# Wq's first half loaded in two slices on two queues, the later slices issued behind the fourth zero matmul

## The chip, the cores and the metric

The kernel runs on one core of one Trainium2 chip. The metric is the device time of one execution in microseconds (us). The profile shows one such execution: its span runs from the first to the last instruction of the program, and the execution's own time is a little longer than the span.

## The reference

Two branches share one input x of 2048 rows and 512 columns, and a gate mixes them:

```python
x = A_x                                               # [1, 2048, 512], bfloat16
g = sigmoid((x * gate_w).sum(-1, keepdims=True))

# branch a: attention, 32 heads of 16, over 8 keys at distances 0, 2, ..., 14 behind each row
q, k, v = split(x @ wqkv)                             # wqkv [512, 1536]
logits  = einsum("bhsd,bhswd->bhsw", q, gathered_k) * 16 ** -0.5
a = einsum("bhsw,bhswd->bhsd", softmax(masked(logits)), gathered_v) @ wo

# branch b: an MLP over the rows
h = layernorm(x)
u = gelu(einsum("bsd,sf->bdf", h, w1) + b1)           # w1 [2048, 1792]
b = (einsum("bdf,fs->bds", u, w2) + b2).transpose     # w2 [1792, 2048]

out = g * a + (1 - g) * b
```

## The kernel before

All work is written as operations with what they read and write, an estimated duration, and one of five queues (SP, POOL, ACT, DVE, PE: SyncE, GpSimd, ScalarE, VectorE, TensorE). A planner (`_Sched`, lines 76 to 279) then puts the operations of each queue into a fixed order by these estimates and works out the semaphore waits. A DMA is an operation of the queue that issues it: an issue time on the queue, and a landing that the planner takes from bytes, or from a due time written by hand (`lands`, line 499). `deps` are waits for completion; `order` and `after` bind only the order in which things are issued. `chain` (line 956) writes parts of the order out by hand, VectorE's among them (line 969).

**TensorE's stages.** Zero matmuls first (`warm1`, line 552: nine of 128x512 into PSUM bank 7, released by a VectorE memset). Then the projections of x to Q, K and V. They contract over 512 columns in four steps (dt 0 to 3), need x transposed (XT, in four blocks of 512 rows, sb 0 to 3) as the moving operand, and columns of Wqkv as the stationary one. One group of four matmuls fills one PSUM bank for one of four column sets (dl 0 to 3), and ScalarE copies the bank out (`ev_...`, lines 651 and 654). The first block of rows is treated apart (lines 656 to 667): Q's four groups go to banks 0 to 3, and K's to banks 4 to 7. Q's are cut by what has landed: dt 0 and 1 over the first 384 rows (XS = 384), dt 0 and 1 over the other 128, dt 2 and 3 over all 512; K's follow whole. After them come the groups of blocks 1 to 3 (`pj_...`, line 678), then V's, all in one order by `after=[last_main[0]]`. All of these matmuls are line 643.

Between them stand bursts of line 698 (`qkr_...`): they sum, over a head's columns, the products q times shifted k that VectorE makes (`qkm_...`, line 690), into banks 4 to 7. `qkr_1_1` reads what `qkm_1_1_0` writes. Behind the projections follows `gz` (line 618), the gate's matmuls, which read a VectorE transpose (`t_b`, line 536); then the MLP's two halves (`ph2`, line 853, and `ph3`, line 890), each ordered behind the one before and behind `gz`; near the end `ws_3` (line 807) and the output projection (`wo`, line 907).

**VectorE's order at the start** is written by hand: memset, an indicator matrix, then the layernorm statistics of row tiles 0 to 3 (`ln1_...`, line 570), the products `qkm_0_0_0` and `qkm_0_1_0`, and so on in turns up to `qkm_1_1_0`, two small operations, `t_b`, and the rest. `ln1_0` needs the first quarter of x in its own layout (`d_x0`).

**The loads at the start.** ACT's queue: Wq's dt 0 and 1 (256 KB, `wq01`), Wq's dt 2 and 3 when the first has landed (`wq23`), Wk whole (512 KB). SP's queue: the transposing DMA of rows 0 to 383 of x (`ld_xt0`, line 484), that of rows 384 to 511 (`xt0b`), the one of block 1 (`ld_xt(1)`, line 477) when `xt0b` has landed, then x's rows 0 to 511 and 512 to 1023 (`ld_x`), blocks 2 and 3 transposed, the rest of x, Wv, w1, wo and the biases. `init_dmas` lists SP's loads, and `throttle()` makes a load wait for the one five places before it in that list.

Of the kernel before, what the change touches and what calls it, by code (L numbers as in the profile page):

```python
# [5 lines left out]
BF16 = mybir.dt.bfloat16  # L6
# [7 lines left out]
D = 512  # L14
# [14 lines left out]
XS = 384  # L29
# [310 lines left out]
def bass_gated_mix__sliding_local_dilated__mixer_token_mlp__prompt_kernel(nc, A_x, A_wqkv, A_wo, B_x, B_w1, B_b1, B_w2, B_b2, gate_w, out, dbg=None):  # L340
    with contextlib.ExitStack() as es:
        block = es.enter_context(nc.Block())
        view, pview, off, total = _views(nc, es)
        ps = es.enter_context(nc.psum_tensor("ps", [128, 8, 512], FP32))
# [34 lines left out]
        OUTS = view("OUTS", BF16, [(D, 4), (1, D)])  # L379
# [51 lines left out]
        A = sch.add  # L431
# [16 lines left out]
        init_dmas = []  # L448
# [15 lines left out]
        def ld_w(tn, d0, n, q="sp"):  # L464
            ds = sch.dsem("wqkv%d_%d" % (tn, d0))
            op = sch.dma(q, mk_dma(WQKV[:, d0:d0 + n, tn * D:(tn + 1) * D], wqkv_v[:, d0:d0 + n, tn * D:(tn + 1) * D]),
                         n * 128 * D * 2, ds, writes=["wqkv%d_%d" % (tn, dt) for dt in range(d0, d0 + n)],
                         deps=throttle() if q == "sp" and n == 4 else [], after=prev_dma() if q == "sp" else [],
                         issue=0.65 if n == 4 else 0.45, name="d_wp%d_%d" % (tn, d0))
            if q == "sp":  # L470
                init_dmas.append(op)
            return op
# [8 lines left out]
        def ld_xt0(s0, s1):  # L481
            ds = sch.dsem("xt0_%d" % s0)
            dst = XT[:, :, s0:s1]
            op = sch.dma("sp", lambda e: e.dma_start_transpose(dst, x2d[s0:s1, :]), (s1 - s0) * D * 2, ds, issue=1.25,
                         writes=["xt_%d" % t for t in range(s0 // 128, s1 // 128)], after=prev_dma(), name="d_xt0_%d" % s0)
            init_dmas.append(op)
            return op

        wq01 = ld_w(0, 0, 2, "act")
        ld_xt0(0, XS)  # L490
        xt0b = ld_xt0(XS, 512)
        wq23 = ld_w(0, 2, 2, "act")
        wq23.deps.add(wq01)
        wk = ld_w(1, 0, 4, "act")
        wk.order.add(wq23)
        ld_xt(1)
        init_dmas[-1].deps.add(xt0b)
        for op_, t_ in ((wq01, 3.0), (init_dmas[0], 4.5), (xt0b, 5.1), (wq23, 5.9), (wk, 7.4), (init_dmas[-1], 9.5)):
            op_.lands = t_
        ld_x(0, 4)  # L500
        ld_x(4, 4)
# [20 lines left out]
        for g in range(4):  # L522
            d_wo = sch.dma("sp", mk_dma(psub(WO, 32 * g, 32, 0, [(D, 4), (1, D)]), wov[g]), 32 * 4 * D * 2, ds_wo,
                           writes=["wo%d" % g], deps=throttle(), name="d_wo%d" % g)
# [6 lines left out]
        for i_, (v_, n_) in enumerate(((B_b1, NFT), (B_b2, NST), (gate_w, 4))):  # L531
            vr = v_.rearrange("(t q j) -> q t j", q=4, j=32)
            for q_ in range(4):
                sch.dma("sp", mk_dma(psub(BR, 32 * q_, n_, 32 * i_, [(1, 32)]), vr[q_]), n_ * 64, ds_b, reads=["br"],
                        writes=["br_%d_%d" % (i_, q_)], deps=throttle(), after=prev_dma(), name="d_b_%d_%d" % (i_, q_), issue=0.45)
        A("dve", lambda e: e.transpose(out=BT, in_=BR), 0.2, reads=["br_%d_%d" % (i_, q_) for i_ in range(3) for q_ in range(4)],
          writes=["gwc"], name="t_b")
        A("act", lambda e: e.activation(out=B1C, in_=BT[:, 0, 0:NFT], func=AF.Copy), 0.2, reads=["gwc"], writes=["b1c"], name="b1c")
        A("act", lambda e: e.activation(out=B2C, in_=BT[:, 1, 0:NST], func=AF.Copy), 0.2, reads=["gwc"], writes=["b2c"], name="b2c")

        WARM = view("OUTS", BF16, [(1, D)], extra=0)
        A("dve", lambda e: e.memset(WARM, 0.0), 0.2, writes=["outs0"], name="warm0")

        def f_warm(n):
            def fn(e):
                ins = None
                for _ in range(n):
                    ins = e.matmul(ps[:, 7, :], lhsT=WARM[:, 0:128], rhs=WARM, start=True, stop=True)
                return ins
            return fn  # L550

        last_tx = A("pe", f_warm(9), 4.0, reads=["outs0"], writes=["lg7_0", "lg7_1"], name="warm1", prio=-100)

        ALLXT = ["xt_%d" % t for t in range(NST)]

# [11 lines left out]
        for hf in range(2):  # L567
            t0 = 8 * hf
            for t in range(t0, t0 + 8):
                A("dve", (lambda t_: (lambda e: e.bn_stats(out=ST6[:, t_, :], in_=X[:, t_, :])))(t), 0.59,  # L570
                  reads=["x%d" % t], writes=["st6_%d" % t], name="ln1_%d" % t, prio=0)
# [13 lines left out]
              reads=["zc%d" % hf], writes=["sd%d" % hf], name="ln_sqrt%d" % hf, prio=0)  # L585
            A("dve", (lambda t0_: (lambda e: e.reciprocal(out=cols(RSTD, t0_, 8), in_=cols(SD, t0_, 8))))(t0), 0.25,
              reads=["sd%d" % hf], writes=["rstd%d" % hf], name="ln_rstd%d" % hf, prio=0)
# [68 lines left out]
        tnames = ["q", "k", "v"]  # L656
        first = [(tn, dl) for tn in range(2) for dl in range(4)]
        fbn = [["acc%d" % b] for b in range(4)] + [["lg%d_0" % b, "lg%d_1" % b] for b in range(4, 8)]
        for (b0, d0, d1, s0, s1) in ((0, 0, 2, 0, XS), (0, 0, 2, XS, 512), (0, 2, 4, 0, 512), (4, 0, 4, 0, 512)):
            for b in range(b0, b0 + 4):  # L660
                tn, dl = first[b]
                last_main[0] = A("pe", f_proj(tn, dl, 0, b, d0, d1, s0, s1), 0.216 * (d1 - d0) * (s1 - s0) / 512,
                                 reads=ALLXT[s0 // 128:s1 // 128] + ["wqkv%d_%d" % (tn, dt) for dt in range(d0, d1)],
                                 writes=fbn[b], after=[last_main[0]], name="pf_%s%d_%d_%d" % (tnames[tn], dl, d0, s0))
        for b, (tn, dl) in enumerate(first):
            A("act", f_evq(tn, dl, 0, b), 0.52, reads=fbn[b] + (["k5pad"] if tn == 1 else []),
              writes=["%s5_%d_0" % (tnames[tn], dl)], name="ev_%s%d_0" % (tnames[tn], dl), prio=0)
# [7 lines left out]
        for (tn, dl, sb) in seq_proj:  # L675
# [3 lines left out]
                             reads=xr + ["wqkv%d_%d" % (tn, dt) for dt in range(4)],  # L679
                             writes=["acc%d" % bank], after=[last_main[0]], name="pj_%s%d_%d" % (tnames[tn], dl, sb), prio=0)  # L680
            A("act", f_evq(tn, dl, sb, bank), 0.62, reads=["acc%d" % bank] + (["k5pad"] if tn == 1 else ["v5pad"] if tn == 2 else []),
              writes=["%s5_%d_%d" % (tnames[tn], dl, sb)], name="ev_%s%d_%d" % (tnames[tn], dl, sb), prio=0)
# [25 lines left out]
        for wh in range(2):  # L708
# [6 lines left out]
            for (dl, c0, nc_) in pieces:  # L715
# [3 lines left out]
                  reads=["q5_%d_%d" % (dl, sb) for sb in range(c0, c0 + nc_)] +  # L719
                        ["k5_%d_%d" % (dl, sb) for sb in range(max(c0 - 1, 0), c0 + nc_)] + ["k5pad"],  # L720
                  writes=wr, name="qkm_%d_%d_%d" % (wh, dl, c0), prio=0)
                if c0 + nc_ == 4 and dl % 2 == 1:
# [4 lines left out]
                    else:  # L727
                        for wl in range(4):
                            qop = A("pe", f_qkr(prs, (wl,)), 0.5, reads=rd, writes=["lg%d_0" % (4 + wl), "lg%d_1" % (4 + wl)],
                                    name="qkr_%d_%d_%d" % (wh, dl, wl), prio=-100 + wl, delay=BURST_DELAY)  # L730
                            A("act", (lambda wh_, wl_: (lambda e: e.activation(out=LGB[:, 4 * wh_ + wl_, :], in_=ps[:, 4 + wl_, :], func=AF.Copy)))(wh, wl),  # L731
                              0.55, reads=["lg%d_0" % (4 + wl), "lg%d_1" % (4 + wl)], writes=["lw%d" % (4 * wh + wl)],
                              name="lev_%d_%d" % (wh, wl), prio=0)
# [24 lines left out]
        for hf in range(2):  # L758
# [3 lines left out]
              reads=["outs1"], writes=lw(hf), name="sm_sub%d" % hf, prio=0)  # L762
            if hf == 0:
                A("act", lambda e: e.activation(out=col(SD, 0), in_=col(ZC, 0), func=AF.Exp, scale=0.0), 1.5,
                  reads=["zc0"], writes=["sd0"], name="sm_pre")
            A("act", (lambda hf_: (lambda e: e.activation(out=ATT[:, 4 * hf_:4 * hf_ + 4, :], in_=LGB[:, 4 * hf_:4 * hf_ + 4, :],  # L766
                                                          func=AF.Exp)))(hf), 1.95,
              reads=lw(hf), writes=["att%d" % hf], name="sm_exp%d" % hf, prio=0)
# [10 lines left out]
        for hf in range(2):  # L779
# [3 lines left out]
              reads=["rs"], writes=["att%d" % hf], name="sm_nrm%d" % hf, prio=0)  # L783
# [3 lines left out]
        for c in range(4):  # L787
            for dh_hi in range(4):
# [4 lines left out]
                               reads=["v5_%d_%d" % (dl, sb) for dl in range(4) for sb in range(4)] + ["v5pad"],  # L793
                               writes=["v3_%d_%d" % (c, dh_hi)], deps=pb2_readers, name="d_v3_%d_%d" % (c, dh_hi)))
# [22 lines left out]
        for t in range(4):  # L817
            tb = []
            for wh in range(2):
# [3 lines left out]
                  writes=["pv%d_%d" % (buf, k_) for k_ in range(4)] + [qk_res, k_res, ["pb0_0", "pb0_1", "m4_0", "m4_1", "m2_0", "m2_1", "m1", "rs"]][buf],  # L823
                  name="avm_%d_%d" % (t, wh))
            b0, b1 = tb
            for (nm, o_, i_, n_, res) in (("ava", b0, b1, 4, None), ("avb", b0, b0, 2, 2), ("avc", b0, b0, 1, 1)):
# [4 lines left out]
                  writes=["pv%d_%d" % (o_, k_) for k_ in range(n_)], name="%s_%d" % (nm, t))  # L831
            if t < 3:
                ds_ot = sch.dsem("ot%d" % t)
                for c in range(4):
                    for g in range(4):
                        sch.dma("sp", mk_dma(psub(OT, 32 * g, 32, t * S + 512 * c, [(1, SC)]),
                                             psub(PV[b0], 32 * c, 32, g * SC, [(1, SC)])), 32 * SC * 2, ds_ot, issue=0.62,
                                reads=["pv%d_0" % b0], writes=["ot%d_%d_%d" % (t, c, g)], deps=v3_ops, name="d_ot%d_%d_%d" % (t, c, g))
            else:
                A("pe", f_ws(b0), 0.45, reads=["pv%d_0" % b0, "ident"], writes=LGA, name="ws_%d" % t, prio=-100, delay=BURST_DELAY)  # L840
                for c in range(4):
                    A("act", (lambda t_, c_: (lambda e: e.activation(out=OT[:, t_, 512 * c_:512 * c_ + 512], in_=ps[:, 4 + c_, :], func=AF.Copy)))(t, c),
                      0.55, reads=["lg%d_0" % (4 + c), "lg%d_1" % (4 + c)], writes=["ot%d_%d_%d" % (t, c, g) for g in range(4)], deps=v3_ops,
                      name="oev_%d_%d" % (t, c), prio=0)
# [13 lines left out]
        for ft in range(NFT):  # L858
            j = ft // 2
            bank = main_bank()  # L860
            for qt in range(4):
                last_main[0] = A("pe", f_ph2(ft, bank, qt), 0.864, reads=["x%d" % t for t in range(4 * qt, 4 * qt + 4)] + ["w1s%d" % (j % 3)],
                                 writes=["acc%d" % bank], after=[last_main[0]], name="ph2_%d_%d" % (ft, qt), prio=0)
            A("act", (lambda ft_, bank_: (lambda e: e.activation(out=UT[:, ft_, :], in_=ps[:, bank_, :], func=AF.Gelu_apprx_tanh,  # L864
                                                                bias=col(B1C, ft_))))(ft, bank), 0.72,
              reads=["acc%d" % bank, "b1c"], writes=["ut%d" % ft] + ALLXT,
              name="gel_%d" % ft, prio=0)
# [206 lines left out]
```

## Time and profile before

| what | value |
|---|---|
| median of 3 runs | 171.72 us (171.43 to 172.06) |
| profiled execution, its own time | 171.57 us |
| its span | 169.8 us, 2216 instructions |
| TensorE clock granted | 1.000 |
| TensorE matmul | 165.2 us busy (97%) |
| VectorE | 142.2 us busy (84%) |
| ScalarE | 76.3 us busy (45%) |
| DMA | 26.97 MB, mean 159 GB/s |

When each load of the start was issued (start of its issue) and landed, in us from the span's start:

| load | queue | issued | landed |
|---|---|---|---|
| Wq, dt 0 and 1 | ACT | 0.80 | 3.56 |
| x transposed, rows 0 to 383 | SP | 0.80 | 5.17 |
| x transposed, rows 384 to 511 | SP | 2.27 | 5.62 |
| Wq, dt 2 and 3 | ACT | 3.58 | 7.22 |
| Wk | ACT | 3.99 | 8.62 |
| x transposed, block 1 | SP | 5.63 | 10.55 |
| x, rows 0 to 511 | SP | 8.44 | 13.18 |

How to read it: a busy TensorE counts matmuls that overlap in its pipeline; a matmul of 512 columns counts 0.379 us, and the next one starts 0.216 us after it (0.163 us for 384 columns, 0.056 us for 128). A line of the profile names start, length, engine, line of the program, operation, what is written from what is read, and in brackets the idle time ahead of it with what ended it. A "q" behind an engine is its instruction queue, where DMAs are issued; among the DMA queues, q1 is the one that SP issues to, and q10 the one of ACT.

### The profile page before, as it was taken

To read this page: it belongs to the slowest core of one execution; us is meant where nothing else is said; L and a number is where in the kernel's file an instruction comes from. 1 tells how busy PE (TensorE), PEld (TensorE's weight loads), DVE (VectorE), ACT (ScalarE), POOL (GpSimd) and SP (SyncE) were. 2 spreads that over 40 slices of the span, in tenths; PEclk is the share of its full clock that TensorE was granted. 3 is DMA by queue.
4 is the path that set the end of the run, shared out by engine and by line. 5 is a ranking of instruction groups with operands and counts; after the bars stand their busy time and mean duration, and the time that the engine had idled before them with its cause. 6 is when DMAs were issued, how large, how long until landed. Compare 5 with 4: busy or idle time off the path is not lost.

```text
span 169.8 us, 2216 instructions
## 1 busy us (share of the span) xinstructions
PE 165.2 (97%) x881; PEld 76.6 (45%) x881; DVE 142.2 (84%) x108; ACT 76.3 (45%) x116; POOL 1.0 (1%) x9
## 2 busy tenths in 40 slices
PE   7999999999999999999999999999999999999992
PEld 2555555544444444444444444444444444444440
DVE  1008999999999973899999999999999999906694
ACT  0476798898979818793111221231312313153000
POOL 2000000000000000000000000000000000000000
PEclk9999999999999999999999999999999999999999
DMA  6999999980004499999999212173777491001443
GB/s 145 260 283 232 303 322 231 239 214 6 0 0 100 96 131 135 253 211 290 294 290 290 68 31 55 36 222 88 201 209 207 105 258 51 0 0 62 143 164 129
DMA packets 50818, 26.97 MB, mean 159 GB/s; under 512 B 12404, under 2 KB 50804, under 8 KB 50808
## 3 DMA queue, kind: packets, MB, share of 16 engines
q1 hardware_dynamic: 49736, 25.78, 63.4%
q10 hardware_dynamic: 1072, 1.05, 2.2%
q8 instruction: 7, 0.11, 0.3%
q14 instruction: 3, 0.02, 0.0%
HBM read 18.89 MB, written 2.11 MB: 124 GB/s over the span
## 4 chain that ended last, share of the span: by engine, by line
PE 94%; DMA 4%; DVE 0%; issue 0%
PE ps L853 29%; PE ps L890 29%; PE ps L643 24%; PE ps L907 8%; PE ps L698 4%; DMA arena<-in_A_wqkv_dram 4%; PE ps L618 1%; DVE arena L919 0%; PE ps L807 0%
## 5 line engine op out<-in xcount | busy, mean ns | idle before, releaser
L853 PE MATMUL ps<-arena 128*128 128x512 bf16 x224 | 48.7, 379 | 0.0
L890 PE MATMUL ps<-arena 128*128 128x512 bf16 x224 | 48.7, 379 | 0.0
L643 PE MATMUL ps<-arena 128*128 128x512 bf16 (+2 forms) x200 | 42.2, 371 | 0.4 <-DMA arena<-in_A_x_dram 0.3
L690 DVE TENSOR_TENSOR arena<-arena 128x4096 bf16<-128x4096 bf16 (+1 forms) x12 | 35.7, 2993 | 0.0
L800 DVE TENSOR_TENSOR arena<-arena 128x8192 bf16<-128x8192 bf16 x8 | 35.1, 4420 | 0.1
L853 PEld LDWEIGHTS ps<-arena 128*128 128x128 bf16 x224 | 21.7, 98 | 26.8 <-issue 0.8
L890 PEld LDWEIGHTS ps<-arena 128*128 128x128 bf16 x224 | 21.9, 98 | 26.4 <-issue 0.2
L828 DVE TENSOR_TENSOR arena<-arena 128x8192 bf16<-128x8192 bf16 (+2 forms) x12 | 31.8, 2647 | 0.4
L643 PEld LDWEIGHTS ps<-arena 128*128 128x128 bf16 x200 | 22.0, 113 | 20.6 <-issue 0.9
L944 ACT ACTIVATE arena<-ps,arena 128x512 bf16<-128x512 f32 x16 | 12.5, 779 | 33.8 <-PE ps L890 33.8
L654 ACT ACTIVATE arena<-ps 128x512 bf16<-128x512 f32 x32 | 18.9, 596 | 5.6 <-PE ps L643 5.4
L864 ACT ACTIVATE arena<-ps,arena 128x512 bf16<-128x512 f32 x14 | 9.6, 687 | 23.9 <-PE ps L853 23.7
L570 DVE BATCH_NORM_STATS2 arena<-arena 128x6 f32<-128x512 bf16 x16 | 10.0, 680 | 11.5 <-DMA arena<-in_A_x_dram 11.5
L919 DVE SCALAR_TENSOR_TENSOR arena<-ps,arena 128x512 bf16<-128x512 f32 x16 | 11.6, 748 | 7.5 <-PE ps L907 5.4
L907 PE MATMUL ps<-arena 128*128 128x512 bf16 x64 | 14.0, 379 | 0.0
L651 ACT ACTIVATE arena<-ps 128x512 bf16<-128x512 f32 x16 | 9.0, 596 | 4.0 <-PE ps L643 4.0
L907 PEld LDWEIGHTS ps<-arena 128*128 128x128 bf16 x64 | 6.3, 98 | 7.5
L594 ACT ACTIVATE arena<-arena 128x512 bf16<-128x512 bf16 x12 | 9.1, 803 | 0.0
L748 DVE TENSOR_TENSOR arena<-arena 128x512 bf16<-128x512 bf16 (+3 forms) x10 | 7.1, 718 | 0.8 <-ACT arena L766 0.5
L698 PE MATMUL ps<-arena 128*32 128x512 bf16 x128 | 7.6, 380 | 0.0
L731 ACT ACTIVATE arena<-ps 128x512 bf16<-128x512 f32 x8 | 4.1, 603 | 2.5 <-PE ps L698 2.5
L698 PEld LDWEIGHTS ps<-arena 128*32 128x32 bf16 x128 | 3.0, 96 | 4.3 <-issue 0.4
(44 smaller groups left out, 36.5 us busy)
## 6 DMA issues: line engine op xcount, KB each, us to landing
arena<-in_B_w_dram SPq DMA_DIRECT2D x7, 1024.0 KB, 9.1
arena<-in_B_w_dram SPq DMA_DIRECT2D x8, 896.0 KB, 5.5
arena<-arena SPq DMA_DIRECT2D x16, 131.5 KB, 3.8
arena<-in_A_x_dram SPq DMA_DIRECT2D x4, 512.0 KB, 5.2
out_dram<-arena SPq DMA_DIRECT2D x16, 128.0 KB, 1.7
arena<-arena SPq DMA_DIRECT2D x48, 32.0 KB, 2.0
arena<-in_A_wqkv_dram ACTq DMA_DIRECT2D x2, 256.0 KB, 3.2
arena<-in_A_wqkv_dram ACTq DMA_DIRECT2D x1, 512.0 KB, 4.6
```

Source lines behind the costliest of these rows:

```text
L570: A("dve", (lambda t_: (lambda e: e.bn_stats(out=ST6[:, t_, :], in_=X[:, t_, :])))(t), 0.59, reads=["x%d" % t], writes=["st6_%d" % t], nam ...
L643: ins = e.matmul(ps[:, bank, s0:s1], lhsT=lhsT, rhs=XT[:, dt, sb * 512 + s0:sb * 512 + s1], start=(dt == 0 and s0 == 0), stop=(dt == 3))
L654: return lambda e: e.activation(out=dst, in_=ps[:, bank, :], func=AF.Copy)
L690: return lambda e: e.tensor_tensor(out=PBL[buf][:, :, 512 * c0:512 * (c0 + nc_)], in0=in0, in1=in1, op=ALU.mult)
L698: ins = e.matmul(ps[32 * c:32 * c + 32, 4 + wl, :], lhsT=RP, rhs=PBL[buf][:, wl, c * 512:(c + 1) * 512], start=(dl == 0), stop=(dl == 3), ...
L800: return lambda e: e.tensor_tensor(out=PV[buf], in0=in0, in1=in1, op=ALU.mult)
L828: A("dve", (lambda o__, i__, n__, f__: (lambda e: e.tensor_tensor(out=PV[o__][:, 0:n__], in0=PV[o__][:, 0:n__], in1=PV[i__][:, f__:f__ + n ...
L853: ins = e.matmul(ps[:, bank, :], lhsT=W1W[:, slot, st, 128 * e_:128 * e_ + 128], rhs=X[:, st, :], start=(st == 0), stop=(st == NST - 1))
L890: ins = e.matmul(ps[:, bank, :], lhsT=W2S[slot][:, ft, 128 * e_:128 * e_ + 128], rhs=UT[:, ft, :], start=(ft == 0), stop=(ft == NFT - 1))
L907: ins = e.matmul(ps[:, WB(i), :], lhsT=OT[:, t, 128 * i:128 * i + 128], rhs=WO[:, t, :], start=(t == 0), stop=(t == 3))
L919: A("dve", (lambda i_: (lambda e: e.scalar_tensor_tensor(out=OUTS[:, i_ % 4, :], in0=ps[:, WB(i_), :], scalar=col(G, i_), in1=T1[:, i_, :] ...
L944: A("act", (lambda i_, bank_: (lambda e: e.activation(out=T1[:, i_, :], in_=ps[:, bank_, :], func=AF.Identity, scale=col(OMG, i_), bias=co ...
```

## The change

Wq's dt 0 is loaded alone on ACT's queue (128 KB) and dt 1 on SP's queue between the two transposing DMAs of block 0. Wq's dt 2 and 3 wait for the first four zero matmuls in place of the first slice's landing. Wk goes in two DMAs of 256 KB. The nine zero matmuls stay, as four and five with a signal between them, and their code moves up in the file. The first projections are cut by dt as the loads are: dt 0 over 384 rows, dt 1 over 384 rows, both over the other 128 rows, dt 2 and 3, and for K dt 0 and 1, then 2 and 3. The due times written by hand change with it.

```diff
--- before.py
+++ after.py
@@ -486,16 +486,33 @@
             init_dmas.append(op)
             return op
 
-        wq01 = ld_w(0, 0, 2, "act")
-        ld_xt0(0, XS)
+        WARM = view("OUTS", BF16, [(1, D)], extra=0)
+        A("dve", lambda e: e.memset(WARM, 0.0), 0.2, writes=["outs0"], name="warm0")
+
+        def f_warm(n):
+            def fn(e):
+                ins = None
+                for _ in range(n):
+                    ins = e.matmul(ps[:, 7, :], lhsT=WARM[:, 0:128], rhs=WARM, start=True, stop=True)
+                return ins
+            return fn
+
+        warm_a = A("pe", f_warm(4), 1.7, reads=["outs0"], writes=["lg7_0", "lg7_1"], name="warm_a", prio=-100)
+        A("pe", f_warm(5), 2.1, reads=["outs0"], writes=["lg7_0", "lg7_1"], after=[warm_a], name="warm_b", prio=-100)
+
+        wq0 = ld_w(0, 0, 1, "act")
+        xt0a = ld_xt0(0, XS)
+        wq1 = ld_w(0, 1, 1)
         xt0b = ld_xt0(XS, 512)
         wq23 = ld_w(0, 2, 2, "act")
-        wq23.deps.add(wq01)
-        wk = ld_w(1, 0, 4, "act")
-        wk.order.add(wq23)
+        wq23.deps.add(warm_a)
+        wk0 = ld_w(1, 0, 2, "act")
+        wk0.order.add(wq23)
+        wk1 = ld_w(1, 2, 2, "act")
+        wk1.order.add(wk0)
         ld_xt(1)
         init_dmas[-1].deps.add(xt0b)
-        for op_, t_ in ((wq01, 3.0), (init_dmas[0], 4.5), (xt0b, 5.1), (wq23, 5.9), (wk, 7.4), (init_dmas[-1], 9.5)):
+        for op_, t_ in ((wq0, 2.6), (xt0a, 4.2), (wq1, 4.4), (xt0b, 5.2), (wq23, 5.8), (wk0, 6.9), (wk1, 7.6), (init_dmas[-1], 9.5)):
             op_.lands = t_
         ld_x(0, 4)
         ld_x(4, 4)
@@ -537,19 +554,6 @@
           writes=["gwc"], name="t_b")
         A("act", lambda e: e.activation(out=B1C, in_=BT[:, 0, 0:NFT], func=AF.Copy), 0.2, reads=["gwc"], writes=["b1c"], name="b1c")
         A("act", lambda e: e.activation(out=B2C, in_=BT[:, 1, 0:NST], func=AF.Copy), 0.2, reads=["gwc"], writes=["b2c"], name="b2c")
-
-        WARM = view("OUTS", BF16, [(1, D)], extra=0)
-        A("dve", lambda e: e.memset(WARM, 0.0), 0.2, writes=["outs0"], name="warm0")
-
-        def f_warm(n):
-            def fn(e):
-                ins = None
-                for _ in range(n):
-                    ins = e.matmul(ps[:, 7, :], lhsT=WARM[:, 0:128], rhs=WARM, start=True, stop=True)
-                return ins
-            return fn
-
-        last_tx = A("pe", f_warm(9), 4.0, reads=["outs0"], writes=["lg7_0", "lg7_1"], name="warm1", prio=-100)
 
         ALLXT = ["xt_%d" % t for t in range(NST)]
 
@@ -656,7 +660,7 @@
         tnames = ["q", "k", "v"]
         first = [(tn, dl) for tn in range(2) for dl in range(4)]
         fbn = [["acc%d" % b] for b in range(4)] + [["lg%d_0" % b, "lg%d_1" % b] for b in range(4, 8)]
-        for (b0, d0, d1, s0, s1) in ((0, 0, 2, 0, XS), (0, 0, 2, XS, 512), (0, 2, 4, 0, 512), (4, 0, 4, 0, 512)):
+        for (b0, d0, d1, s0, s1) in ((0, 0, 1, 0, XS), (0, 1, 2, 0, XS), (0, 0, 2, XS, 512), (0, 2, 4, 0, 512), (4, 0, 2, 0, 512), (4, 2, 4, 0, 512)):
             for b in range(b0, b0 + 4):
                 tn, dl = first[b]
                 last_main[0] = A("pe", f_proj(tn, dl, 0, b, d0, d1, s0, s1), 0.216 * (d1 - d0) * (s1 - s0) / 512,

```

## The prediction

> **What bounds the kernel now.** I read the page first, then the chain of waits in order of time, then the first 15 us and the moments around 51 us instruction by instruction. The page's line of the chain that ended last:
>
> ```profile
> PE 94%; DMA 4%; DVE 0%; issue 0%
> ```
>
> TensorE sets the end. The pieces of that chain (start, length, what) say where DMA's 4% is:
>
> ```profile
> 0.80 2.76 DMA arena<-in_A_wqkv_dram
> 3.56 0.02 issue
> 3.58 3.64 DMA arena<-in_A_wqkv_dram
> 7.22 0.05 issue
> 7.27 26.95 PE ps L643 x124
> ...
> 51.10 1.84 PE ps L698 x32
> ```
>
> Everything that the change touches lies ahead of 7.27 us; behind it TensorE runs without a hole. The reader is to see that the chain goes through two loads of Wq, the second issued when the first has landed. The timeline of the start (start, length, queue or engine) shows the other load that is waited for:
>
> ```profile
> 0.80 2.72 SPq L484 DMA_TRANSPOSE arena<-in_A_x_dram  x2
> 0.80 3.68 ACTq L446 DMA_DIRECT2D arena<-in_A_wqkv_dram  x3
> 1.25 3.74 PE L548 MATMUL ps<-arena 128*128 128x512 bf16 x9 [1.25 <-DVE arena L542]
> 5.30 0.98 PE L643 MATMUL ps<-arena 128*128 128x384 bf16 x5 [0.31 <-DMA arena<-in_A_x_dram]
> 5.63 2.76 SPq L477 DMA_TRANSPOSE arena<-in_A_x_dram  x1
> ```
>
> The first projection starts at 5.30, released by the transpose of the first 384 rows (issued 0.80, 4.4 to landing: 5.17). The other 128 rows land at 5.62 (2.27 + 3.35), Wq's second half at 7.22 (3.58 + 3.64), Wk at 8.6 (3.99 + 4.6). Of idle on TensorE that a faster start could remove there are thus 0.31 us ahead of 5.30, plus what an earlier landing gives, and 0.21 us ahead of 7.27.
>
> The chain hides a second one that runs level with it. VectorE, and then TensorE with VectorE around 51 us:
>
> ```profile
> 13.21 2.47 DVE L570 BATCH_NORM_STATS2 arena<-arena 128x6 f32<-128x512 bf16 x4 [11.52 <-DMA arena<-in_A_x_dram]
> ...
> 46.38 4.42 DVE L690 TENSOR_TENSOR arena<-arena 128x8192 bf16<-128x8192 bf16 x1
> ...
> 51.03 0.27 DVE L536 STREAM_TRANSPOSE arena<-arena 128x96 bf16<-128x96 bf16 x1
> 51.03 0.40 PE L698 MATMUL ps<-arena 128*32 128x512 bf16 x4
> ```
>
> VectorE starts when the first quarter of x lands (issued 8.44, 4.7 to landing) and is then busy 37.26 of the 37.50 us from 13.20 to 50.70; the rest are gaps of 0.03 between dependent instructions. The product that ends at 50.80 (qkm_1_1_0) is read by the burst at 51.03 (qkr_1_1). From the warm-up I have what such a hand-over takes: the memset ends at 1.195, the first matmul starts at 1.253, 0.06. So the burst could have started at 50.86: **0.17 us of slack.** The earlier bursts have more (34.15 against 33.46 + 0.06: 0.63; 41.30 against 40.83 + 0.06: 0.41), the one at 63.34 has 0.82. Nor can the plan put other work ahead of the burst at 51.03: the next main work is gz, which reads the VectorE transpose of L536, behind the same product, and every ph2 is ordered behind gz. So **TensorE past 51 us gains at most 0.17 us plus whatever VectorE gains**, and VectorE hangs on a chain of SP: landing of the 128 rows, issue of xt1 (5.63, 2.76 long), issue of x0 (8.44), its landing (13.18).
>
> **The change, part by part.** I write d for how much later the 128 rows (xt0b), and with them x0 and VectorE, come; g for how much earlier TensorE gets.
>
> *Half a slice less ahead of the transpose.* Wq's first slice shrinks from 256 to 128 KB. By queue, from 2.6 to 3.2 us (packets, MB, share of 16 engines):
>
> ```profile
> q10 hardware_dynamic: 154, 0.14, 68.0%
> q1 hardware_dynamic: 231, 0.06, 43.3%
> ```
>
> q10 is ACT's, q1 SP's. In a finer cut q1 has nothing until 2.7 and then grows as q10 dies away: the engines are full, and the transpose waits for Wq's tail. From 5.9 to 7.2 q10 alone moved 357 GB/s, so 131 KB are 0.37 us: that is the most the 384 rows can gain. The least is 0, if their descriptors are not there sooner. Its first packets came at 2.7 at the earliest, on average over the engines at about 2.95; if all could start at 2.7 the gain is 0.25, which I take. First projection at 5.05 (bounds 4.93 to 5.30; the ninth zero matmul, started at 4.61 with 0.22 to the next, allows 4.83).
>
> *The second slice in SP's queue.* One issue more on SP (0.43, as ACT's of 256 KB) between the transposes; the second transpose's issue moves from 2.27 to 2.7 and still lies under the first one's data. Its data cost xt0b the 0.37 again, since the queue moves in order: d = -0.25 + 0.37 = +0.12 so far. For TensorE the slice lands at most 0.4 after the 384 rows, and is wanted 4 x 0.163 = 0.65 after: hidden.
>
> *Wq's second half on the fourth zero matmul.* That matmul starts at 2.51 and ends at 3.14, so the issue goes from 3.58 to 3.14, 0.44 earlier. Its first packets, at 4.7 before, would come at 4.27, and now meet wq1 and xt0b, which have until 5.0 + 0.12. Before, from 4.7 to 5.55, the same first 0.85 us of q10 moved 0.09 MB (90 packets, slow ones), 0.26 us at 357 GB/s. Bounds 0 and 0.26 on d; I take 0.15, since these packets wait more than they move (157 GB/s in all). Then **d = +0.27**, lands 5.89, where TensorE wants it at 5.05 + 1.30 = 6.35: hidden. The half itself: 7.22 - 0.44, plus some 0.2 behind q1, 6.98; wanted at 5.05 + 1.30 + 0.45 = 6.80. Wk's projections then begin at 6.98 + 0.05 + 8 x 0.216 = 8.76 instead of 9.02: **g = 0.26.**
>
> *The rest costs nothing, with its cover.* Wk in two DMAs is one more issue of about 0.4 on ACT; the four end near 4.5 as the three did (4.48), ahead of the table load (4.51 to 5.79), and ACT's first evictions come at 7.93: 2.1 us of cover. wk0 is half of what took 1.4 us after Wq's half (7.22 to 8.6), so it lands near 7.7, before 8.76; wk1 follows at 8.4, wanted at 10.5. The nine zero matmuls stay nine; the quarters are the same matmuls (8 x 384 columns, 16 of Wk) in another order, with two waits more. Wk's first bank is now complete 0.9 us later, since the halves go round all four banks; its reader on VectorE starts at 15.59 and needs also the eviction of sb 1, which follows by 15.0, so that is covered. xt1 lands at 10.55 + 0.27 and is wanted at 12.47 - 0.26: 1.4 of cover left. xt2 (16.56) is wanted at 19.4 and xt3 (18.79) at 20.2.
>
> *The sum.* TensorE brings -0.26 to the burst at 51.03, VectorE +0.27 against a slack of 0.17: the later of them is +0.27 - 0.17 = **+0.10**. Past that burst nothing is nearer (VectorE ends at 148.55, wanted at 150.97). The profiled execution took 171.57, its span 169.8; it becomes 171.67. The median of the runs is 171.72, 0.15 over it, so I say **171.8**. Bounds of the terms: d from -0.37 + 0.37 = 0 (then -0.17) to 0.37 + 0.26 = +0.63 (then +0.46): 171.5 to 172.2.
>
> **Rivals.**
> *A, slower: Wq's second half takes half of the engines from xt0b.* Place: from 4.27 until SP's queue has drained, at 5.12 if left alone; it decides when q10 flows at full rate from its first packet. q10 has 0.79 MB waiting, 2.2 us, so for 0.85 us of SP's data the two share evenly and xt0b ends up to 0.85 late; I take 0.7. d = +0.82, minus 0.17: +0.65, 172.4. For it: two queues did fill the engines together from 2.6 to 3.2. Against it: q10's slow first packets. The Trainium skill (DMA: Bandwidth & Descriptors, "Queues, rings and completion order") says that each DMA engine goes round its queues packet by packet, which is this rival, and its "Rules for kernel authors" that spreading loads over SP and ACT brings no bandwidth. The row from 2.6 to 3.2 agrees in part: both move, though not evenly.
>
> *B, held back: q10 waits until q1 has drained.* From 4.7 to 5.0 q10 came in just as q1 went out. Then the earlier issue gains nothing, d = +0.12, TensorE's g is near 0: -0.05, 171.7.
>
> *C, faster: x0 comes earlier.* From 7.2 to 8.1 q10 still moved 0.16 MB of Wk, 0.45 us, beside xt1. If the earlier issue takes that away and xt0b is at its lower bound, d = -0.45, and TensorE's own gain is then 9.02 - (4.93 + 1.75 + 1.73) = 0.61: up to -0.61, 171.1; halfway 171.4. Against it: xt1's packets from 8.1 to 8.4, with q10 gone, were no faster.
>
> **How the numbers follow.** Chances: forecast 0.37, A 0.29, B 0.16, C 0.18. 0.3% is 0.52 us, about what a measurement of this kernel can tell from no change (the runs spread over 0.6). Faster by more: most of C, 0.15. Slower by more: A but its small end, 0.25, and 0.03 of the forecast: 0.28. Within: 0.57. The range reaches into A and C: 171.2 to 172.5.
>
> **What would show it.** Right: the first matmul of L643 near 5.05, xt1's issue on SP near 5.9, VectorE's first instruction near 13.5, and VectorE's L690 named as what ended an idle time of TensorE ahead of L698 near 51.1. Each number is one step. Wrong: VectorE starting at 13.2 or before with the burst ahead of 50.9 (then C), xt1's issue at 6.3 or later (A), or any time ahead of 7 us that reaches the end in full, which would mean that the second chain isn't there.

## The result and the profile after

The changed kernel takes **173.07 us** (median of 6 runs, 173.00 to 173.28) against 171.57 for the kernel before (6 runs, 171.36 to 172.30): a ratio of **1.0084, 95% interval 1.0067 to 1.0101**. It is slower, and outside the predicted range. The profiled execution took 173.19, its span is 171.5 instead of 169.8. To the nanosecond the spans are 171.469 and 169.848, so **1.62 us** have to be found.

The line of the chain that ended last, from the page of the kernel after (shares of the span by engine):

```profile
PE 67%; DVE 22%; DMA 6%; SPq 2%; issue 1%
```

TensorE's 94% have become 67%, and VectorE, which had 0%, has 22%. Where the chain changes engine is seen in its pieces, in order of time (start, length, what; SPq is SP issuing a DMA). L694 is L690 of before, L702 is L698 and L574 is L570: the lines have moved by four.

```profile
2.87 5.31 DMA arena<-in_A_x_dram
8.18 0.02 issue
8.20 1.92 SPq L477
10.11 0.05 issue
10.16 4.82 DMA arena<-in_A_x_dram
14.98 0.02 issue
15.00 2.47 DVE arena L574 x4
...
52.65 1.91 PE ps L702 x32
```

The reader is to see the second chain of the prediction, link by link: the transpose of the 128 rows (xt0b, issued 2.87) lands at 8.18, then SP issues xt1, then x0, which lands at 14.98, then VectorE starts, and TensorE meets it at the burst at 52.65. Before, the same moments were 5.62, 13.18, 13.21 and 51.03.

The start of the kernel after, lines picked from the timeline (start, length, queue or engine, in brackets the idle time before and what ended it):

```profile
2.25 0.56 SPq L446 DMA_DIRECT2D arena<-in_A_wqkv_dram  x1
2.87 1.20 SPq L484 DMA_TRANSPOSE arena<-in_A_x_dram  x1
5.05 0.81 PE L647 MATMUL ps<-arena 128*128 128x384 bf16 x4
6.12 0.84 PE L647 MATMUL ps<-arena 128*128 128x384 bf16 x4 [0.25 <-DMA arena<-in_A_wqkv_dram]
8.22 7.98 PE L647 MATMUL ps<-arena 128*128 128x128 bf16 x41 [1.26 <-DMA arena<-in_A_x_dram]
```

The first projection does start at 5.05 (before 5.30); the 384 rows land at 4.47 (before 5.17). Then TensorE stands still twice: 0.25 for the second slice of Wq (landed 6.07), and 1.26 for the 128 rows. K's projections begin at 10.43 instead of 9.02. So both chains are late: TensorE by 1.41, VectorE by 1.80 (15.00 against 13.21 in the timelines). The burst moves from 51.028 to 52.653, by 1.625, which is 1.80 less the 0.17 of slack, and the whole span moves by the same 1.62. Wq's second half, issued at 3.18 instead of 3.58, lands at 7.93 instead of 7.22.

How the data of the 128 rows went is in the DMA view of the kernel after, from 5.4 to 6.4 us (packets, MB, share of the 16 engines' time that the queue's packets took; q10 is ACT's, q1 SP's):

```profile
DMA packets 210, 0.13 MB, mean 128 GB/s; under 512 B 112, under 2 KB 210, under 8 KB 210
...
q10 hardware_dynamic: 100, 0.10, 98.3%
q1 hardware_dynamic: 110, 0.03, 26.3%
```

In this window the two queues move about as many packets as each other, 100 and 110 (from 4.7 to 5.55 it was 39 and 235). By the time that they took, one packet of Wq's half lasted 0.983 x 16 x 1.0 us / 100 = 157 ns, against 0.263 x 16 / 110 = 38 ns for one of the transpose. The two shares add up to 125%, so packets overlap in time, and a packet's time is not time in which its engine can do nothing else. The Trainium skill (DMA: Bandwidth & Descriptors, "Queues, rings and completion order") says that each DMA engine goes round its queues a packet at a time. The like counts of this window agree with it, but they do not prove it: the records do not name the engine of a packet, and a packet of the profile (256 or 1024 bytes here) need not be what the Trainium skill calls one, which is several descriptors long. That the transpose goes at the pace of its slow neighbour, some 7 of its packets on each engine in 1 us, is therefore argued, not shown. The data end at about 6.6, and from 6.6 to 6.95 the view has no row for q1 at all. From 6.95 to 7.25 it shows:

```profile
q10 hardware_dynamic: 113, 0.10, 108.2%
q1 hardware_dynamic: 26, 0.00, 5.4%
```

The 26 packets of q1 without bytes to speak of I read as the transpose's reports of its end: in the packet records of the traces they have 4 bytes, and each transpose has 32 of them, each plain load 16. The landing at 8.18 follows 1.0 us behind the last of them (7.19); in the kernel before it was 0.6 (5.04 and 5.62).

### The profile page after: what moved, and what is told of

The parts are those of the page before. It is cut to its first block, busy times and chain, and to the rows that moved or that the text cites. A ratio compares the mean times of both kernels' runs of the same rounds, so it can differ in the third digit from the quotient of the medians.

```text
span 171.5 us, 2203 instructions
## 1 busy us (share of the span) xinstructions
PE 164.2 (96%) x866; PEld 76.6 (45%) x881; DVE 142.1 (83%) x108; ACT 76.0 (44%) x116; POOL 1.0 (1%) x9
## 4 chain that ended last, share of the span: by engine, by line
PE 67%; DVE 22%; DMA 6%; SPq 2%; issue 1%
PE ps L857 28%; PE ps L894 28%; DVE arena L694 15%; PE ps L911 8%; DMA arena<-in_A_x_dram 6%; DVE arena L574 6%; PE ps L702 2%; SPq L477 1%; SPq L484 1%; PE ps L622 1%; DVE arena L923 0%; SPq L446 0%; PE ps L811 0%; DVE arena L582 0%; DVE arena L578 0%
## 5 line engine op out<-in xcount | busy, mean ns | idle before, releaser
L894 PE MATMUL ps<-arena 128*128 128x512 bf16 x219 | 48.2, 379 | 0.4 <-issue 0.2
L857 PE MATMUL ps<-arena 128*128 128x512 bf16 x219 | 48.1, 379 | 0.5 <-issue 0.3
L694 DVE TENSOR_TENSOR arena<-arena 128x4096 bf16<-128x4096 bf16 (+1 forms) x12 | 35.7, 2992 | 0.0
L574 DVE BATCH_NORM_STATS2 arena<-arena 128x6 f32<-128x512 bf16 x16 | 10.1, 680 | 13.3 <-DMA arena<-in_A_x_dram 13.3
L911 PE MATMUL ps<-arena 128*128 128x512 bf16 x63 | 13.9, 379 | 0.1
L702 PE MATMUL ps<-arena 128*32 128x512 bf16 x128 | 7.6, 380 | 0.1
L496 PE MATMUL ps<-arena 128*128 128x512 bf16 x9 | 4.0, 625 | 1.3 <-DVE arena L490 1.3
```

What stands on the lines that cost most here:

```text
L694: return lambda e: e.tensor_tensor(out=PBL[buf][:, :, 512 * c0:512 * (c0 + nc_)], in0=in0, in1=in1, op=ALU.mult)
L702: ins = e.matmul(ps[32 * c:32 * c + 32, 4 + wl, :], lhsT=RP, rhs=PBL[buf][:, wl, c * 512:(c + 1) * 512], start=(dl == 0), stop=(dl == 3), ...
L857: ins = e.matmul(ps[:, bank, :], lhsT=W1W[:, slot, st, 128 * e_:128 * e_ + 128], rhs=X[:, st, :], start=(st == 0), stop=(st == NST - 1))
L894: ins = e.matmul(ps[:, bank, :], lhsT=W2S[slot][:, ft, 128 * e_:128 * e_ + 128], rhs=UT[:, ft, :], start=(ft == 0), stop=(ft == NFT - 1))
L911: ins = e.matmul(ps[:, WB(i), :], lhsT=OT[:, t, 128 * i:128 * i + 128], rhs=WO[:, t, :], start=(t == 0), stop=(t == 3))
```

## The experiments

Each kernel was timed beside the kernel before in the same session (its median there was 171.77 or 171.79, 171.53 or 171.47); ratios are against that, with their 95% interval. Landing times are those of one profiled execution, which need not be a typical one, and a ratio is over all runs. In the profiles of the six kernels whose loads up to the 128 rows are those of the kernel before (before, e4, e5, e8, e9, e10) these rows land at 5.62 to 6.05, 5.82 in the mean; a difference of 0.4 us between two single profiles thus tells nothing. The first group takes one part of the change alone, the second leaves the change whole and moves the moment of Wq's second half.

**e3_early_alone: the kernel before, and of the change only the trigger.**

```
-        wq23.deps.add(wq01)
+        wq23.deps.add(warm_a)      # warm_a: the first four zero matmuls
+        wq23.order.add(wq01)
```

> The kernel before with one edit, Wq's dt 2 and 3 issued when four zero matmuls are done; Wq's first half stays one load on ACT's queue. 'Interleaving': ACT's packets begin near 4.5 while SP's queue drains at 5.0, so the 128-row transpose lands 0.3 to 2 late (5.9 to 7.6), VectorE starts as much later, time 171.7 to 173.1. 'Slice': it lands at 5.6 as before, Wq's half at 6.8, TensorE's K projections at 8.7; time 171.3 to 171.5, no more than the slack of 0.17 better.

172.46 (171.57 to 173.40, 10 runs), ratio 1.0032 [1.0011, 1.0053]. The 128 rows land at 7.37, 1.75 late (1.3 against the latest of the six), with nothing ahead of them in SP's queue that wasn't there before. Wq's half gains 0.09 from an issue 0.41 earlier (3.17, landed 7.13). The chain of waits of this kernel's first 16 us, then its timeline:

```profile
2.25 5.11 DMA arena<-in_A_x_dram
...
7.38 1.78 SPq L477
...
9.21 5.07 DMA arena<-in_A_x_dram
```

```profile
0.80 2.82 SPq L484 DMA_TRANSPOSE arena<-in_A_x_dram  x2
...
7.41 8.84 PE L645 MATMUL ps<-arena 128*128 128x128 bf16 x45 [0.35 <-DMA arena<-in_A_x_dram]
...
14.30 1.88 DVE L572 BATCH_NORM_STATS2 arena<-arena 128x6 f32<-128x512 bf16 x3 [12.62 <-DMA arena<-in_A_x_dram]
```

It is the chain of the whole change in small. VectorE starts 1.10 late, the burst is 0.92 late (51.945), and 1.10 less the slack of 0.17 is 0.93. The trigger alone brings about a loss of this kind, though a smaller one than the whole change (0.32% against 0.84%); e11 below, with the same trigger, has the rows nearly as late and loses nothing that can be measured.

**e4_wk_halves_alone: the kernel before with Wk in two loads, and K's projections by halves.**

```
-        wk = ld_w(1, 0, 4, "act")
+        wk0 = ld_w(1, 0, 2, "act")
+        wk1 = ld_w(1, 2, 2, "act")
-        ... (4, 0, 4, 0, 512)):
+        ... (4, 0, 2, 0, 512), (4, 2, 4, 0, 512)):
```

> The kernel before with Wk in two DMAs and K's projections by halves of the contraction, nothing else. Both theories: the 128-row transpose lands at 5.6, VectorE starts at 13.2, time 171.4 to 171.8, the same as before. If the extra DMA of ACT is a cause of its own, x's first quarter lands 0.3 or more later and the time follows.

171.82, ratio 1.0001 [0.9985, 1.0017]. This part costs nothing that can be measured, as predicted.

**e1_fifth, e6_sixth: the change, with the trigger on the fifth and on the sixth zero matmul.**

```
-        warm_a = A("pe", f_warm(4), ...   A("pe", f_warm(5), ... after=[warm_a]
+        warm_a = A("pe", f_warm(5), ...   A("pe", f_warm(4), ...        # e1
+        warm_a = A("pe", f_warm(6), ...   A("pe", f_warm(3), ...        # e6
```

> The changed kernel with Wq's dt 2 and 3 waiting for five zero matmuls in place of four (issue near 3.60 in place of 3.18, as in the kernel before). Theory 'interleaving' (the 128-row transpose is late because ACT's loads reach the DMA engines before SP's queue has drained, and each engine then takes turns between one slow packet of theirs and one of the transpose): the first packets of ACT's load move from 4.6 to about 5.0, the transpose drains by 5.3 and lands at 5.8 to 6.6 in place of 8.18; time 171.3 to 171.9. Theory 'slice' (a plain load between two transposes in SP's queue is what slows the second, whatever ACT does): it lands at 8.0 to 8.2 again, time 173.0 to 173.2.

> The changed kernel with Wq's dt 2 and 3 waiting for six zero matmuls (issue near 4.05). 'Interleaving': ACT's first packets come near 5.5, when the 128-row transpose has some 50 packets left at most; it lands near 6.1 as in the run in which nothing of ACT's meets it (6.06), Wq's half at 7.6, K's projections begin at 9.4 (0.35 later than before), time 171.8 to 172.2. Were it instead the split of Wq over the two queues that costs, the 128 rows would land at 7 or later again as with five (7.09), time 172.5.

Issued at 3.60 (e1): 172.55, ratio 1.0037 [1.0019, 1.0055]; the 128 rows land at 7.09, Wq's half at 7.15. That is later than the theory of a meeting had (5.8 to 6.6, and 171.9 at most): at 3.60 the loads still meet. The profiled execution was the quickest of its ten (171.89), and in it x0 lands only 0.26 late. Issued at 4.03 (e6): 172.12, ratio 1.0015 [0.9998, 1.0033]; the 128 rows land at **5.95**, Wq's half at 7.79. The timeline of e6:

```profile
5.97 3.06 SPq L477 DMA_TRANSPOSE arena<-in_A_x_dram  x1
7.83 8.39 PE L647 MATMUL ps<-arena 128*128 128x512 bf16 x37 [1.11 <-DMA arena<-in_A_wqkv_dram]
```

With the meeting nearly gone (31 packets of the transpose's data were left when the load's first came) the wait for the rows is gone too, and TensorE waits 1.11 for Wq's half instead. K begins at 9.56, 0.54 late, and the burst at 51.595, 0.57 late, with VectorE's product done at 50.97: here TensorE sets the end.

**e2_wait_xt0b: the change, with Wq's second half held until the 128 rows have landed.**

```
-        wq23.deps.add(warm_a)
+        wq23.deps.add(xt0b)
```

> The changed kernel with Wq's dt 2 and 3 issued when the 128-row transpose has landed, so that nothing of ACT's meets it. 'Interleaving': it lands at 5.6 to 6.0, VectorE starts at 13.2 to 13.7; but Wq's half is issued at 5.7 and lands at 9.0 or later, so TensorE's K projections start near 10.8 in place of 9.0, and the time is 173 to 174 by TensorE. 'Slice': the transpose lands at 6.5 or later.

173.58, ratio 1.0101 [1.0079, 1.0124]. The timeline:

```profile
6.08 3.11 SPq L477 DMA_TRANSPOSE arena<-in_A_x_dram  x1
9.38 6.88 PE L647 MATMUL ps<-arena 128*128 128x512 bf16 x30 [2.26 <-DMA arena<-in_A_wqkv_dram]
```

The rows land at 6.06, so 2.1 us of their lateness in the changed kernel come from the meeting with Wq's half. The 0.44 that is left against the kernel before, with the slice ahead of them, is no more than the six profiles above differ by. The kernel as a whole loses more: Wq's half lands at 9.34, and its traffic now meets xt1 (landed 12.91 instead of 10.55) and x0 (VectorE at 14.25). It shows the price of waiting for good, not a cure.

**e7_one_queue: the change, with everything behind the first slice in SP's queue, in the order of use, and no waits among them (block 1 is also freed from `throttle()`).**

```
-        wq23 = ld_w(0, 2, 2, "act")
-        wq23.deps.add(warm_a)
+        wq23 = ld_w(0, 2, 2)
...
-        init_dmas[-1].deps.add(xt0b)
```

> The changed kernel with everything behind Wq's dt 0 in SP's queue in the order of use, with no wait between: 384 rows, dt 1, 128 rows, dt 2 and 3, Wk's halves, block 1, x. Nothing interleaves and no load waits for a landing or a matmul. 'Interleaving' (what costs is packets of two queues taking turns, the bytes are the same): 128 rows land at 5.9 to 6.1, Wq's half at 6.8 to 7.2, Wk near 8.3, VectorE starts at 11 to 12.5 in place of 13.2, K's projections at 8.6 to 9.0; time 171.0 to 171.5, below both kernels. If the plain loads between transposes in one queue are what costs, the transposes come later than before here too and the time is 172 or more.

172.15, ratio 1.0018 [1.0001, 1.0035]. The rows land at 5.97, as expected. Wq's half (issued 4.13) lands at 7.41, Wk at 8.51 and 9.20: later than expected, and x0 comes at 13.11, hardly sooner than before. One queue keeps the order and takes away the meeting, but a plain load takes its 3.3 us to land there as well (7.41 - 4.13), and nothing is gained on the kernel before.

**e5_vector_later: is the second chain there? The kernel before, with two more bn_stats on VectorE ahead of the first.** They repeat statistics that are computed again right behind.

```
+            for k_ in range(2 if hf == 0 else 0):
+                A("dve", lambda e: e.bn_stats(out=ST6[:, 0, :], in_=X[:, 0, :]), 0.59, ...
```

> The kernel before with the statistics of row tile 0 made three times over in place of once on VectorE (two more of 0.59 ahead of ln1_0), nothing else; no load moves. If VectorE is level with TensorE up to the burst near 51 us with 0.17 of slack, 1.19 more on VectorE costs 1.19 - 0.17 = 1.0 us: span 170.8 to 170.9, the burst waits for VectorE. If TensorE alone sets the end, and the landing of the 128 rows costs only through its own matmuls, the time stays 171.4 to 171.9.

172.62, ratio 1.0043 [1.0020, 1.0065], span 170.887: 1.04 longer, where 1.0 was expected. The timeline at the burst:

```profile
47.59 4.42 DVE L693 TENSOR_TENSOR arena<-arena 128x8192 bf16<-128x8192 bf16 x1
52.06 0.61 PE L701 MATMUL ps<-arena 128*32 128x512 bf16 x8 [0.17 <-DVE arena L693]
```

VectorE's product ends at 52.004 (before 50.796, so 1.21 later), and the burst starts 0.055 behind it, 1.03 late. That it is so near to the 1.0 is in part luck: x0 landed 0.25 sooner here, and the two more took 1.46 instead of 1.19. The two chains run level to 0.17 us, and what VectorE loses beyond that reaches the end.

**e11_early_dt2_first, e12_early_wk_first: what in the meeting delays the rows?** Two explanations were left: the slow first packets of whichever plain load comes (*slow start*), or the rows being tied to the end of the load that they meet (*tied*). e11 is e3 with Wq's half as two loads, the smaller one first; e12 is e3 with all of Wk ahead of Wq's half.

```
+        wq2 = ld_w(0, 2, 1, "act")      # e11; wq2.deps.add(warm_a)
+        wq3 = ld_w(0, 3, 1, "act")
...
+        wk.deps.add(warm_a)             # e12
+        wq23.order.add(wk)
```

> The run 'early alone' (the kernel before, Wq's second half issued when four zero matmuls are done) with that half in two loads of 128 KB, dt 2 and dt 3. In three runs so far where ACT's load met the 128-row transpose both landed within 0.25 of each other (7.93 and 8.18; 7.15 and 7.09; 7.13 and 7.37). Theory 'tied' (the transpose's completion is held until the ACT load that met it has completed): it now lands with dt 2, 0.4 or more earlier than 7.37, at 6.2 to 6.9. Theory 'slow start' (it is held while the first packets of ACT's queue are slow, until 6.0, however large the load): 7.1 to 7.5 again.

> The run 'early alone' with Wk (512 KB) in front of Wq's second half on ACT, both otherwise the same. 'Tied': the 128-row transpose lands with Wk, at 7.9 to 8.8, later than 7.37. 'Slow start': at 7.0 to 7.6, though ACT's first load runs on to 8. By either, Wq's half lands last, near 8.6, so that TensorE comes at least 1.4 late and the time is above 173.

With the small load in front the rows land at 7.20 (the load at 6.96; 171.76, ratio 1.0005 [0.9986, 1.0024]), with the large one at 7.09 (the load at 7.75; 172.78, not above 173, ratio 1.0065 [1.0040, 1.0090]), against 7.37 in e3. The size of the load shows no effect, as *slow start* had it. It is e12 that speaks against *tied*; in e11 the small load came so late that the two again land within 0.25 of each other. The timeline of e12:

```profile
7.10 1.77 SPq L477 DMA_TRANSPOSE arena<-in_A_x_dram  x1
8.50 7.74 PE L645 MATMUL ps<-arena 128*128 128x512 bf16 x34 [0.73 <-DMA arena<-in_A_wqkv_dram]
```

xt1 is issued at 7.10, released by the rows, while Wk, the load that they met, is still coming until 7.75. e12 loses its time through Wq's half, which lands at 8.45 (TensorE 1.23 late at 8.50 against 7.27, the burst at 52.26 likewise).

A third explanation fits every profile and was not tested: that the *issues* meet, not the data. In the five profiles in which the rows land at 7.09 or later (the changed kernel, e1, e3, e11, e12), ACT issues its load while SP is still issuing the 128-row transpose: at 3.18 within 2.87 to 4.07 in the changed kernel, at 3.60 within 2.88 to 4.08 in e1, at 3.18 within 2.25 to 3.62 in e3. In the other nine (5.62 to 6.06) it does so behind that (before: 3.58 against 3.51), in its last 0.04 us (e6), or not at all (e7). The data still to come divide the two groups less well: when the load's first packet comes, 89 and 117 packets of the transpose's data are left in e11 and e12, whose rows are late, and 90, 129 and 159 in the kernel before, e8 and e9, whose rows are not. So *slow start* is not shown as the reason; what is shown is that the early load makes the rows late.

**e8_x_first, e9_wq_thirds, e10_x_first_thirds: could the two chains be pulled forward?** e8 is the kernel before with x0 ahead of xt1 in SP's queue, e9 the kernel before with the two slices of Wq's second half as separate loads, each with its own projections, and e10 has both.

```
+        x0 = ld_x(0, 4)                 # e8: ahead of ld_xt(1)
+        x0.deps.add(xt0b)
...
-        wq23 = ld_w(0, 2, 2, "act")     # e9
+        wq2 = ld_w(0, 2, 1, "act")
+        wq3 = ld_w(0, 3, 1, "act")
-        ... (0, 2, 4, 0, 512),
+        ... (0, 2, 3, 0, 512), (0, 3, 4, 0, 512),
```

> The kernel before with one edit: x's first quarter is issued on SP ahead of block 1 of the transposes (both when the 128 rows have landed). VectorE's statistics start near 10 in place of 13.2, its products at 15.1 in place of 15.6 (then bound by the eviction of K's block 1, which ends near 15.0), so the second chain gains 0.5 and the slack at the burst near 51 becomes 0.6 to 0.7; block 1 lands at 11.4 to 12.3, wanted at 12.47. If VectorE's late start is what spreads the runs of the kernel before (171.4 to 172.4), the runs now lie closer together near the lower end: median 171.3 to 171.6. If TensorE's own loads spread them, the median stays at 171.7 to 171.8.

> The kernel before with Wq's dt 2 and dt 3 in two loads, one behind the other on ACT, and Q's projections cut so. dt 2 lands 0.3 ahead of dt 3, TensorE's idle of 0.21 ahead of them goes, K's projections begin at 8.8 in place of 9.02. By VectorE's chain the end gains no more than 0.17: median 171.6 to 171.8. If TensorE alone set the end it would be 171.5 or less.

> Both edits: x's first quarter ahead of block 1, and Wq's dt 2 and dt 3 in two loads. With VectorE relieved TensorE's 0.2 reaches the end: median 171.1 to 171.4, below each edit alone and below the kernel before by 0.2 to 0.4%. If the gains don't add, the median is that of the better of the two.

e8: 171.95, ratio 1.0012 [0.9996, 1.0027]; e9: 171.92, 1.0010 [0.9994, 1.0025]; e10: 172.15, 1.0030 [1.0015, 1.0045]. All three miss. In e8 VectorE starts at 9.87, 3.3 us earlier, yet the burst is at 51.53: TensorE sets it, and TensorE was itself slower (last section). In e9 dt 2 lands at 6.09 and dt 3 at 6.42 and TensorE's idle is gone, as expected, but its first matmuls were slow here too, and K begins at 9.34, 0.32 late; Wk slips from 8.62 to 9.14, which still is in time for that. In e10 they were slow as well, xt1 comes at 13.20, and TensorE waits 0.54 for it. No version beat the kernel before.

## Why the prediction was wrong

- **Right: the second chain and its slack.** VectorE's lateness less 0.17 is the burst's lateness in the changed kernel (1.80, 1.625), in e3 (1.10, 0.92) and, taken at the product's end, in e5 (1.21, 1.03).
- **Right: the halves of Wk cost nothing** (e4).
- **Right by luck: the first projection at 5.05.** By the sum the 384 rows set it, landing 0.25 earlier, 0.37 at most. They landed 0.70 earlier, at 4.47, and the ninth zero matmul set the start: it began at 4.64 and held the next one off for 0.41, where the prediction had 0.22 (4.83 at the earliest).
- **Wrong, and the step that failed: "Wq's second half on the fourth zero matmul".** The prediction put "0.15" on d for it, with "Bounds 0 and 0.26". Alone (e3) it makes the 128 rows **1.75 us late** (1.58 and 1.47 in e11 and e12); in the changed kernel it is about 2.1 (8.18 against 6.06 in e2). The price was made from bytes: 0.09 MB at 357 GB/s are 0.26 us. The row of before from 4.7 to 5.55 that it was read from has a third column:

```profile
q10 hardware_dynamic: 90, 0.09, 76.6%
...
q1 hardware_dynamic: 193, 0.04, 28.6%
```

  By time, q10's 90 packets took 0.766 x 0.85 = 0.65 us of all engines: 116 ns a packet, against 20 ns for one of q1's. "These packets wait more than they move" was read as room for the transpose, and there was no such room. But 0.65 is far too small as well. Of the 2.1 us, 1.0 are in the transpose's data (the last packet starts at 6.58, in e2 at 5.57), 0.6 in its reports (the last at 7.19 and 5.59), and 0.5 lie between these and the landing. Whether slow packets that take turns bring this about, or the issues that overlap, stays open.
- **Wrong with it: "lands 5.89 ... hidden" and g = 0.26.** TensorE wanted the rows at 6.35 by the sum; they came at 8.18, the cover was gone, and TensorE was 1.41 late by K's projections instead of 0.26 early. Had VectorE alone been in time, the burst would still have been at about 51.03 + 1.41 = 52.44 (worked out, not run).
- **Too small: the slice in SP's queue, 0.37.** With the slice, and Wq's half out of the way (e2, e6, e7), the landings of the 384 and of the 128 rows stand 1.20 to 1.39 apart; in the six profiles without it 0.45 to 0.84. In the mean that is 0.7 more, where its bytes give 0.37. But the 384 rows come 0.5 earlier in these runs, where the sum took 0.25, so that the 128 rows are only 0.2 late in the mean (5.95 to 6.06 against 5.62 to 6.05), which cannot be told from the sum's 0.12. The second slice was also not "hidden": TensorE waited 0.25 for it.
- **Not one to one: d and VectorE.** The sum let VectorE be as late as the rows. xt1's issue takes up part of it: 2.76 long before, 1.92 after, 1.78 in e3. What is left varies with x0's own landing: rows 2.56 late, VectorE 1.80 (after); 1.75 and 1.10 (e3); 1.47 and 0.26 (e1); 1.58 and 0.12 (e11). What sets the last part stays open.
- **The rivals.** A had the place and the sign, and its sign to look for (xt1's issue at 6.3 or later; it came at 8.20), but its price of up to 0.85 was again made from bytes shared evenly: 172.4 instead of 173.07. C did not happen. Of B one half shows in e3: issued 0.41 earlier, Wq's half has its first packet at 4.82, no earlier than before (4.76), and gains only 0.09 in landing. But B left the rows alone, and they are late.
- **How the loss divides.** Ratios: trigger alone 1.0032, the rest with a late trigger (e6) 1.0015 and not to be told from none, Wk's halves 1.0001, all together 1.0084. They do not add up: what the trigger costs depends on the slice. The pair that shows it is e1 and the kernel before. Wq's half is issued at 3.60 and 3.58; the rows land at 7.09 with the slice ahead of them and at 5.62 without it (e1's halves of Wk leave them at 6.05 in e4). The slice keeps the transpose under way longer, its issue until 4.08 instead of 3.51 and its data too; which of the two counts is open. Later triggers shrink the rows' loss (landing 8.18, 7.09 and 5.95 with the fourth, fifth and sixth matmul).

Three things stay open: whether it is the packets or the issues whose meeting delays the transpose; why the first packets of a plain load are so slow, also where the load is alone (in the kernel before, from 5.1 to 5.35, q10's 21 packets took 110.9% of that time, 211 ns each, without one of q1's); and why the transpose's reports come as late as 7.1 when its data are through at 6.6.

## What to carry to other kernels

Do not price a transfer that shares the DMA engines by its bytes: here 0.26 us by bytes stood for 1.5 to 2.1 us of another transfer's landing. The time that its packets take (share times span, 0.65 us here) came nearer and was still too small, so such a term needs a wide range, or a run. An earlier issue of a load need not land it earlier (0.41 us brought 0.09), and it can cost the transfer that everything else hangs on more than 2 us; ask first who is still under way, the issue included. And where two engines run level (0.17 us here), a delay that the first can hide must be followed through the second one to its end.

## What the runs showed of the hardware that was not expected

**TensorE's first matmuls ran at half rate in some executions, with the granted clock shown as 1.00.** The first projections of e8, from the view of that line's instructions from 5.2 to 6.5 us (count, duration in ns as min/median/max, first and last start), and then the same of the kernel before:

```profile
L644 PE MATMUL ps<-arena x4: 482/524/524, 5.3 to 6.2; 128*128 128x384 bf16 x4
```

```profile
L643 PE MATMUL ps<-arena x7: 326/326/327, 5.3 to 6.3; 128*128 128x384 bf16 x7
```

Both begin at 5.30. In e8 the second starts 0.278 behind the first, the next four 0.320 apart, and the rest 0.163, as all do in the kernel before; e9, e10 and e11 have four slow ones each. In e8 these are 0.115 + 4 x 0.157 = 0.74 us, of which a later wait takes up some: the burst is 0.51 late (51.53 against 51.03). It may be a part of the spread of the kernel before (171.4 to 172.3). The mean granted clock of both executions is 1.000, but the clock records in the traces begin only with the moment at which the full clock is granted: 4.57 in the kernel before, 6.86, 6.54, 6.50 and 6.92 in e8 to e11, and the matmuls become fast there. The views show 1.00 ahead of it too. The Trainium skill (TensorE: Matmul & The Clock Gate, "What's actually happening") says that the window on which the clock is opened runs freely and does not start with the kernel, so that the moment shifts by some 0.5 us; the two rows, the same matmuls from the same start at unlike rates, agree with it. The changed kernel spreads over only 0.28 us: its early waits for loads are longer than this difference, which fits, but was not tested.

**An issue of a DMA on SP got shorter when it came later:** with the order of SP's queue as it was before, xt1's took 2.35 to 3.35 us when it began at 5.6 to 6.1 (seven profiles, the kernel before among them), and 1.77 to 1.99 from 7.1 to 8.2 (five, the changed kernel among them).
